# First-batch chunks, one early fold, a split load and an earlier order of steps at the head of a fused attention and feed-forward kernel

## The chip, the cores and the metric

One NeuronCore of a Trainium2 chip runs the whole program. The metric is device time in microseconds, the median of several executions. One of these executions is recorded by the hardware profiler; its trace and page are what is read here. PE is the matrix engine (PEld its weight loads), DVE the vector engine, ACT the scalar engine, POOL the GpSimd engine, which issues most of the loads here, and SP the queue that issues stores and transposes.

## The reference

Four batches of 6080 tokens with 256 channels go through a channel attention, then all 24320 tokens through a feed-forward layer of 2048 hidden units:

```
qn = q / (norm(q, axis=tokens) + 1e-6);  kn likewise
s  = kn.T @ qn / tau                      # 256 x 256 for each batch
a  = softmax(s)
x  = v @ a                                # (4*6080, 256)
h  = x @ w_in                             # 256 -> 2048
out = (s*relu(h)**2 + b) @ w_out          # 2048 -> 256
```

Inputs and outputs are float32, `tau` is 1.

## The kernel before

The attention matrix never meets v directly: it is folded into the weights, `wa = a @ w_in` (fp16, 256 x 2048, one for each batch), and then h = v @ wa. So the first batch's matrix must be ready before any feed-forward work can start, and the later batches' matrices are worked out beside the main loop.

**Head (first batch).** q and k are loaded in chunks, `chunks_first`: pairs (partitions, rows per partition). Before, these are eleven chunks of four rows, nine on 128 partitions and those at places 4 and 6 on 120, and two of two rows on 128. The first two come by SP and ACT in float32, the others by POOL, which casts to fp16 on the way. For each chunk PE adds to the Gram matrix `s_ps` (L152), DVE or ACT square q and k (L175 to L181), DVE folds the four squared rows to one (`fold`, L195) and adds them to the first chunk's (`into_first`, L209). The last three chunks (`NLATE`) are kept apart: for these all k loads come first, then all q loads, and their squares are not folded but summed by PE row for row (`unfolded`, `add_norms`, L242 for k, L246 for q). The sums become inverse norms by four ACT operations (L267), `scale` (L292) multiplies the Gram matrix with k's, and `exps` (L298) takes the exponentials. `first_block` works out the first 256 columns of `wa` (L341, L336), `folds` the rest (L325): blocks of 256 columns at 256, 512 and 768, and of 512 at 1024 and 1536, each in two halves m = 0 and 1. Each half is scaled out of PSUM by ACT (L318) or DVE (L320): m = 0 by ACT, but by DVE for the blocks at 512 and 768; m = 1 always by DVE.

POOL issues the loads in this order: k and q, the first group of v (`load_v(0)`), `w_in` in four loads (two halves of its first 512 columns, columns 512 to 1024, columns 1024 to 2048), the second group of v, the four pieces of `w_out`, the third group of v, the scalars. Eight of its loads can be in flight; each further one waits for the landing of the eighth before it.

**Main loop.** A group is 512 tokens; step s = 16 g + m works on hidden columns 128 m to 128 m + 127 of group g. `mm1` (L656) makes these hidden units, two matmuls of 512 columns for two halves of `wa`; two steps share one PSUM tile of `ps_h`, which has two buffers. After every odd step ACT takes the relu of both (`relu`, L666); then comes the square, g = r * r (L679 on DVE, L677 on ACT). Group 0 is `plain`: its output matmuls (L728) start at step 11. The other groups use a scheme with seven products (L824) that needs sums of squares (L751 to L757) on DVE.

The order of the work on each engine is the program's order, which `po` fixes. What stands where around the change:

- `FOLDS` gives the steps after which the eight halves from column 512 on are folded and scaled: 1, 1, 3, 3, 6, 6, 10, 10. Columns from 1024 are first used at step 8, from 1536 at step 12.
- Group 0's first four squares are put on DVE at steps 5, 6, 7 and 8, the others right behind their relu.
- At step 7 DVE casts the first piece of `w_out` (L553), at step 12 PE transposes the second group of v (L395) and DVE copies it (L397); from step 13 on DVE has the sums for the constant row and the combinations of `w_out`.
- `keep_busy` (L474) puts extra matmuls between the chunks of the head.

Of the kernel before, what the change touches and what calls it, by code (L numbers as in the profile page):

```python
# [9 lines left out]
FP16 = mybir.dt.float16  # L10
# [7 lines left out]
def kernel(  # L18
# [12 lines left out]
    nc = tc.nc  # L31
    P = 128

    B, N, C = q.shape
    Dff = moe_w_in.shape[1]
# [20 lines left out]
    def po(ins):  # L56

        tc.keep_in_program_order(ins)
        return ins

    def pool(name, bufs, **kw):
        return ctx.enter_context(tc.tile_pool(name=name, bufs=bufs, **kw))
# [6 lines left out]
    late_pool = pool("late_pool", NLATE)  # L69
# [25 lines left out]
    JC = 4  # L95
    NDIRECT = 2

    NSHORT = 120

    def make_chunks(shapes):  # L100
        chunks, at = [], 0
        for np_, j in shapes:
            chunks.append((at, np_, j))
            at += np_ * j
        assert at == N
        return chunks

    whole, rest = divmod(N, P * JC)
    chunks_later = make_chunks([(P, JC)] * whole + [(rest // JC, JC)])
    short = [(P, JC)] * (whole - 2) + [(P, 2)] * 2  # L110
    for at in (4, 6):
        short.insert(at, (NSHORT, JC))
    chunks_first = make_chunks(short)

    class Gram:

# [44 lines left out]
        def norm_ops(self, c):  # L161

            qc, kc = self.tiles[c]
            _, np_, jc = self.chunks[c]
            st = {}

            at_end = self.b == 0 and c >= len(self.chunks) - NLATE

            def squares(a, js):
                def f():  # L170
                    if "sq" not in st:
                        st["sq"] = (late_pool if at_end else sq_pool).tile(
                            [P, 2, JC, C], FP16, tag="sq", name="sq")
                    if a == 1 and at_end and c == len(self.chunks) - 1:
                        po(nc.vector.tensor_mul(  # L175
                            st["sq"][:np_, 1, js, :], kc[:np_, js, :], kc[:np_, js, :]))
                    elif a == 0 and (self.b > 0 or at_end or c % 2 == 0):
                        po(nc.vector.tensor_mul(  # L178
                            st["sq"][:np_, 0, js, :], qc[:np_, js, :], qc[:np_, js, :]))
                    else:  # L180
                        po(nc.scalar.activation(  # L181
                            out=st["sq"][:np_, a, js, :], in_=(qc, kc)[a][:np_, js, :],
                            func=AF.Square))
                return f

            def fold(half, arrays, last):
                def f():
                    src = st["f", 2 * half] if 2 * half < jc else st["sq"]
                    if ("f", half) not in st:
                        if last:  # L190
                            t = f3_pool.tile([P, 2, 1, C], FP16, tag="f3", name="f3")
                        else:
                            t = sq_pool.tile([P, 2, half, C], FP16, tag=f"f{half}", name="f")
                        st["f", half] = t
                    po(nc.vector.tensor_add(  # L195
                        st["f", half][:np_, arrays], src[:np_, arrays, :half, :],
                        src[:np_, arrays, half : 2 * half, :]))
                    if last and c == 0:
                        self.first = st["f", half]
                    if last and (c == 0 or self.b > 0 and c == len(self.chunks) - 1):  # L200
                        for rows in self.rows:
                            rows.append((st["f", half], np_, 1))
                return f

            def into_first():

                dst, src = self.first[:np_], st["f", 1][:np_]
                if self.b == 0:
                    po(nc.vector.tensor_add(dst, dst, src))  # L209
                else:  # L210
                    po(nc.gpsimd.dma_start(out=dst, in_=src, accum_op=ALU.add))  # L211

            def unfolded(a):
                self.rows[a].append((st["sq"], np_, jc))

            ops = []
            for h in range(0, jc, 4):
                js = slice(h, min(h + 4, jc))
                ops += [squares(1, js), squares(0, js)]
            if at_end:  # L220
                return ops + [unfolded]
            if jc == 8:
                ops += [fold(4, slice(0, 1), False), fold(4, slice(1, 2), False)]
            ops += [fold(2, slice(0, 2), False), fold(1, slice(0, 2), True)]
            return ops + [into_first] if 0 < c < len(self.chunks) - 1 else ops
# [149 lines left out]
    def group(g):  # L375
        t0 = g * TG
        return t0, min(TG, NT - t0) // P
# [60 lines left out]
    NW = 512  # L438
    w_in_rows = moe_w_in.rearrange("(co p) f -> p co f", p=P)

    def load_w_in(f0, f1, co=None):
        cs = slice(0, CH) if co is None else slice(co, co + 1)
        po(nc.gpsimd.dma_start(out=w_in16[:, cs, f0:f1], in_=w_in_rows[:, cs, f0:f1]))
# [2 lines left out]
    for co in range(CH):  # L446
        load_w_in(0, NW, co)
    load_w_in(NW, 2 * NW)
    load_w_in(2 * NW, Dff)
    w_out_rows = moe_w_out.rearrange("(fo p) d -> p fo d", p=P)  # L450
    load_v(1)

# [27 lines left out]
    late = range(NCH0 - NLATE, NCH0)  # L480
    for c in range(NCH0 - NLATE):
        ops = g0.norm_ops(c)
# [3 lines left out]
        if c == NCH0 - NLATE - 1:  # L486
            ops, last_sum = ops[:-1], ops[-1]
# [4 lines left out]
    ops = {c: g0.norm_ops(c) for c in late}  # L492
# [71 lines left out]
    def at_step(s, f):  # L564
        side.setdefault(int(s), []).append(f)
# [1 line left out]

    FIN = (0, 3, 5, 7, 9, 11, 13, 17, 19, 22)
    first_group = [b * N // TG for b in range(B)]
    FOLDS = (1, 1, 3, 3, 6, 6, 10, 10)  # L570
    for i, f in enumerate(folds[2:]):
        early.setdefault(FOLDS[i], []).append(f)
    at_step(14, lambda: po(nc.vector.tensor_scalar_mul(
# [87 lines left out]
    def relu(g, i):  # L661
        n = group(g)[1] * P
        if i % 2 == 0:
            r_tiles[g, i // 2] = rpool.tile([P, 2, 2, TG], FP16, tag="r16", name="r16")
        r16 = r_tiles[g, i // 2]
        po(nc.scalar.activation(out=r16[:, :, i % 2, :n], in_=h_tiles.pop((g, i))[:, :, :n],  # L666
                                func=AF.Relu))

    def square(g, i0, i1, engine):

        n = group(g)[1] * P
        if i0 == 0:
            g_tiles[g] = gpool.tile([P, 2, NP, TG], FP16, tag="g16", name="g16")
        src = r_tiles[g, i0 // 2][:, :, i0 % 2 : i0 % 2 + i1 - i0, :n]
        dst = g_tiles[g][:, :, i0:i1, :n]
        if engine is nc.scalar:
            po(nc.scalar.activation(out=dst, in_=src, func=AF.Square))  # L677
        else:
            po(nc.vector.tensor_mul(dst, src, src))  # L679
# [168 lines left out]
    for s in range(NS + FT):  # L848
        g, m = divmod(s, FT)
        if g < NG:  # L850
            mm1(g, m)
        for f in early.pop(s, []):
            f()

        if m == SHIFT and 0 < g and g - 1 not in plain:
            items = seven_items(g - 1)
            work.append((items, 8 if g == NG - 1 else 7))
        if work:
            items, n = work[0]
            for f in items[:n]:  # L860
                f()
            del items[:n]
            if not items:
                work.pop(0)
        for gp in plain:
            for mp in range(FT):
                if s == gp * FT + PLAG[gp] + (mp * 4 // 3 if gp == 0 else mp):
                    plain_mm2(gp, mp)
        if g < NG and m % 2 == 1:
            relu(g, m // 2)  # L870
            if g in plain:
                late = g > 0 and m // 2 % 2 == 0
                if g > 0 or m >= 9:
                    square(g, m // 2, m // 2 + 1, nc.scalar if late else nc.vector)
        if 5 <= s <= 8:
            square(0, s - 5, s - 4, nc.vector)
        if g < NG and g not in plain and m in SQUARES:
            square(g, *SQUARES[m])
        if g == NG - 1 and m in LAST:
            LAST[m]()  # L880
        elif m == 0 and 0 < g and g - 1 not in plain:
            square(g - 1, 6, 8, nc.vector)
        elif 0 < g and g - 1 not in plain and m in SUMS:
            sums_of(g - 1, SUMS[m])
        for f in side.pop(s, []):
            f()
# [34 lines left out]
```

## Time and profile before

| | |
|---|---|
| median of 4 executions | 719.4 us (719.37 to 719.85) |
| the profiled execution, time | 719.85 us |
| its span, first to last instruction | 718.1 us |
| busy, PE | 695.5 us (97%) |
| busy, DVE / ACT / POOL | 623.0 (87%) / 545.2 (76%) / 109.9 us (15%) |
| granted clock of PE | 1.00 |
| DMA, mean | 116 GB/s; busy share 90% or more in the first 7 of 40 slices |
| first matmul of the feed-forward part (L656) | 38.53 us |

The page divides the span in 40 slices of 18 us. Only the first two are not full for PE: the head is a wait for loads, and the rest is nearly all matmuls. A row of a chain gives a start, a length and what ran; a row of a group gives an engine, what it wrote from what, a count, the busy time and the mean of one.

### The profile page before, as it was taken

The numbers are of one execution on the slowest core, as the hardware profiler recorded it, in microseconds if no ns is written. First come the engines' busy times: TensorE is split into PE (matmuls) and PEld (weight loads), VectorE is DVE, ScalarE is ACT, GpSimd is POOL, SyncE is SP. The second block draws the span as 40 slices with busy tenths as digits, with TensorE's granted clock in tenths as the row PEclk, the third lists the DMA queues.
The fourth block names the chain that finished last, engine by engine and source line by source line (L and its number), as shares of the span: only waits on it lengthen the run. The fifth ranks groups of instructions, "written<-read, shape, count | busy, mean of one in ns | idle before, by whom it ended". The sixth has DMA issues, their size and how long they took to land.

```text
span 718.1 us, 17493 instructions
## 1 busy us (share of the span) xinstructions
PE 695.5 (97%) x7423; PEld 502.8 (70%) x7423; DVE 623.0 (87%) x875; ACT 545.2 (76%) x593; POOL 109.9 (15%) x188
## 2 busy tenths in 40 slices
PE   4599999999999999999999999999999999999998
PEld 2456777776677777777677777777668777777777
DVE  4879999988889999998888899998887888888886
ACT  5779877787777777778777778777877777777875
POOL 4532332201201222111010222110000000000000
PEclk9999999999999999999999999999999999999999
DMA  9999999636555878444773788843323333321201
GB/s 237 204 259 170 152 168 147 111 99 123 107 107 126 141 134 144 108 92 88 134 154 54 147 125 130 155 90 75 99 63 74 94 71 75 96 60 46 82 31 74
DMA packets 86990, 83.47 MB, mean 116 GB/s; under 512 B 56320, under 2 KB 61568, under 8 KB 86912
## 3 DMA queue, kind: packets, MB, share of 16 engines
q0 software_dynamic: 26144, 43.40, 37.5%
q1 hardware_dynamic: 60192, 37.64, 21.4%
q8 instruction: 58, 0.95, 0.6%
q10 hardware_dynamic: 576, 1.31, 0.5%
q14 instruction: 20, 0.16, 0.1%
HBM read 78.91 MB, written 24.90 MB: 145 GB/s over the span
## 4 chain that ended last, share of the span: by engine, by line
PE 92%; DMA 4%; DVE 2%; ACT 1%; POOL 1%; issue 0%; POOLq 0%; ACTq 0%
PE h_ps L656 45%; PE o_ps L824 40%; PE s_ps L152 4%; DMA qk<-in_k_dram 3%; PE wa_ps L325 2%; DMA v<-in_v_dram 1%; PE o_ps L728 1%; DVE g L679 0%; PE o_ps L702 0%; POOL qk L136 0%; ACT r L666 0%; DVE wa L320 0%; DVE o_sb L684 0%; DVE S L753 0%; DVE sq L178 0%
## 5 line engine op out<-in xcount | busy, mean ns | idle before, releaser
L666 ACT ACTIVATE r<-h_ps 128x1024 f16<-128x1024 f32 (+1 forms) x384 | 388.5, 1014 | 152.5 <-PE h_ps L656 148.6
L656 PE MATMUL h_ps<-vT,wa 128*128 128x512 f16 (+7 forms) x1632 | 452.4, 364 | 0.6 <-DVE wa L320 0.4
L824 PEld LDWEIGHTS <-S 128*128 128x128 f16 x2944 | 198.0, 98 | 84.8 <-issue 0.2
L824 PEld LDWEIGHTS <-g 128*128 128x128 f16 x2208 | 155.0, 98 | 74.1
L679 DVE TENSOR_TENSOR g<-r 128x2048 f16<-128x2048 f16 (+2 forms) x150 | 174.4, 1164 | 13.5 <-ACT r L666 12.9
L824 PE MATMUL o_ps<-T,S 128*128 128x128 f16 x2208 | 183.3, 219 | 0.1
L656 PEld LDWEIGHTS <-wa 128*128 128x128 f16 x1632 | 135.8, 98 | 21.2 <-DVE wa L320 1.3
L824 PE MATMUL o_ps<-w_out,g 128*128 128x128 f16 x1472 | 134.2, 219 | 0.2 <-DVE u L684 0.2
L684 DVE SCALAR_TENSOR_TENSOR o_sb<-o_ps,s_out,u 128x256 f32<-128x256 f32 x138 | 66.3, 481 | 50.9 <-PE o_ps L824 48.9
L677 ACT ACTIVATE g<-r 128x1024 f16<-128x1024 f16 (+1 forms) x97 | 100.4, 1035 | 0.2
L152 PE MATMUL s_ps<-qk 128*128 128x256 f16 (+2 forms) x384 | 70.0, 282 | 15.9 <-ACT qk L143 8.9
L384 POOL DMA_DIRECT2D v<-in_v_dram x48 | 31.5, 660 | 265.1 <-DMA vT<-v 214.2
L684 DVE SCALAR_TENSOR_TENSOR u<-o_ps,s_out,rowconst 128x256 f32<-128x256 f32 x138 | 65.8, 477 | 0.0
L824 PE MATMUL o_ps<-w_out,S 128*128 128x128 f16 x736 | 63.4, 219 | 0.0
L824 PE MATMUL o_ps<-N,g 128*128 128x128 f16 x736 | 63.4, 219 | 0.0
L211 POOL DMA_DIRECT2D f<-f x30 | 26.3, 876 | 225.4 <-DVE f L195 175.4
L753 DVE TENSOR_TENSOR S<-S,g 128x2048 f16<-128x2048 f16 (+1 forms) x47 | 56.4, 1201 | 1.3
L181 ACT ACTIVATE sq<-qk 128x1024 f16<-128x1024 f16 (+3 forms) x53 | 54.5, 1042 | 3.9 <-DMA qk<-in_k_dram 2.3
L751 DVE TENSOR_TENSOR S<-g 128x2048 f16<-128x2048 f16 (+1 forms) x47 | 56.0, 1192 | 0.0
L755 DVE TENSOR_TENSOR S<-g 128x2048 f16<-128x2048 f16 x46 | 55.9, 1214 | 0.0
L757 DVE TENSOR_TENSOR S<-g,S 128x2048 f16<-128x2048 f16 x46 | 55.9, 1214 | 0.0
L152 PEld LDWEIGHTS <-qk 128*128 128x128 f16 (+2 forms) x384 | 32.2, 101 | 21.9 <-ACT qk L143 9.4
(81 smaller groups left out, 312.6 us busy)
## 6 DMA issues: line engine op xcount, KB each, us to landing
out_dram<-o_sb SPq DMA_DIRECT2D x42, 512.0 KB, 2.9
v<-in_v_dram POOLq DMA_DIRECT2D x47, 256.0 KB, 4.7
qk<-in_k_dram POOLq DMA_DIRECT2D x40, 256.0 KB, 6.5
qk<-in_q_dram POOLq DMA_DIRECT2D x40, 256.0 KB, 7.5
f<-f POOLq DMA_DIRECT2D x30, 128.0 KB, 3.2
vT<-v SPq DMA_TRANSPOSE x182, 3.1
out_dram<-o_sb SPq DMA_DIRECT2D x10, 256.0 KB, 4.4
w<-in_moe_w_out_dram POOLq DMA_DIRECT2D x4, 512.0 KB, 10.2
```

Source lines behind the costliest of these rows:

```text
L152: po(nc.tensor.matmul(self.s_ps[:, ch, :], qc[:np_, j, ts(ch, P)], kc[:np_, j, :], start=(c == 0 and j == 0 and ch == 0), stop=(c == len(s ...
L181: po(nc.scalar.activation(out=st["sq"][:np_, a, js, :], in_=(qc, kc)[a][:np_, js, :], func=AF.Square))
L656: po(nc.tensor.matmul(dst, wa[:, ci, ts(m, P)], src, start=(ci == 0), stop=(ci == CH - 1), skip_group_check=True))
L666: po(nc.scalar.activation(out=r16[:, :, i % 2, :n], in_=h_tiles.pop((g, i))[:, :, :n], func=AF.Relu))
L677: po(nc.scalar.activation(out=dst, in_=src, func=AF.Square))
L679: po(nc.vector.tensor_mul(dst, src, src))
L684: po(nc.vector.scalar_tensor_tensor(out=dst, in0=src, scalar=s_out, op0=ALU.mult, in1=add, op1=ALU.add))
L751: po(nc.vector.tensor_add(T[1], A21, A22))
L753: po(nc.vector.tensor_sub(T[2], T[1], A11))
L755: po(nc.vector.tensor_sub(T[3], A11, A21))
L757: po(nc.vector.tensor_sub(T[4], A12, T[2]))
L824: po(nc.tensor.matmul(st[name][:, j, :], a()[:, i, ts(j, P)], w[:, i, :], start=first, stop=last, skip_group_check=True))
```

## The change

Four edits, all in the head and in the first ten steps of the main loop:

- `make_chunks` now takes the rows per partition alone and puts each chunk on 128 partitions while rows last. The first batch's chunks become eleven of four rows and one of two rows on 128 partitions, and a last one of two rows on 96. The later batches' chunks stay as they are.
- Of the three last chunks, the one with four rows gets a fold of its squares, once for k and once for q: DVE adds rows 0 and 1 to rows 2 and 3 in a new tile `h`, and PE sums two rows in place of four. In DVE's order k's add stands ahead of the last chunk's k square, q's add ahead of the two other q squares.
- `w_in`'s last 1024 columns come in two loads of 512.
- The blocks at 1024 and 1536 are folded at steps 5 and 8 instead of 6 and 10, and group 0's squares all stand right behind their relu, so the first four at steps 1, 3, 5 and 7. At step 5 the block's scaling thereby stands ahead of the step's relu on ACT.

PE's program has 12 instructions fewer (four ahead of the first late chunk's Gram matmuls, eight behind them), ACT's and DVE's work in the main loop is the same but in another order, POOL has one more load.

```diff
-    NSHORT = 120
-
-    def make_chunks(shapes):
+    def make_chunks(rows_of):
         chunks, at = [], 0
-        for np_, j in shapes:
+        for j in rows_of:
+            np_ = min(P, (N - at) // j)
             chunks.append((at, np_, j))
             at += np_ * j
...
-    whole, rest = divmod(N, P * JC)
-    chunks_later = make_chunks([(P, JC)] * whole + [(rest // JC, JC)])
-    short = [(P, JC)] * (whole - 2) + [(P, 2)] * 2
-    for at in (4, 6):
-        short.insert(at, (NSHORT, JC))
-    chunks_first = make_chunks(short)
+    whole = N // (P * JC)
+    chunks_first = make_chunks([JC] * whole + [2, 2])
+    chunks_later = make_chunks([JC] * (whole + 1))
...
+            if at_end and jc == 2:
+                return ops + [unfolded]
             if at_end:
-                return ops + [unfolded]
+                def half(a):
+                    if "h" not in st:
+                        st["h"] = late_pool.tile([P, 2, 2, C], FP16, tag="h", name="h")
+                    po(nc.vector.tensor_add(st["h"][:np_, a], st["sq"][:np_, a, :2],
+                                            st["sq"][:np_, a, 2:]))
+                    self.rows[a].append((st["h"], np_, 2))
+                return ops + [half]
...
-    load_w_in(2 * NW, Dff)
+    load_w_in(2 * NW, 3 * NW)
+    load_w_in(3 * NW, Dff)
...
-    FOLDS = (1, 1, 3, 3, 6, 6, 10, 10)
+    FOLDS = (1, 1, 3, 3, 5, 5, 8, 8)
...
                 late = g > 0 and m // 2 % 2 == 0
-                if g > 0 or m >= 9:
-                    square(g, m // 2, m // 2 + 1, nc.scalar if late else nc.vector)
-        if 5 <= s <= 8:
-            square(0, s - 5, s - 4, nc.vector)
+                square(g, m // 2, m // 2 + 1, nc.scalar if late else nc.vector)
```

## The prediction

> **What bounds the kernel now.** I read the busy shares by slice first, then the chain of waits with its pieces in order of time, then stretches cut at the chain's turning points, and last the timeline of DVE around steps 6 to 12.
>
> Stretches (PE, PEld, DVE, ACT, POOL busy us with counts, clock, DMA share, GB/s):
>
> ```profile
> 30.00:34.77 4.77, 3.71 (x44) 2.73 (x42) 2.99 (x7) 3.55 (x8) 3.74 (x6) 1.00 1.16 201
> 34.77:36.58 1.81, 0.00 (x0) 0.01 (x1) 0.75 (x2) 1.48 (x5) 0.27 (x1) 1.00 1.22 200
> 36.58:43.47 6.89, 6.89 (x48) 4.04 (x49) 4.13 (x10) 4.30 (x7) 3.66 (x6) 1.00 1.09 287
> 43.47:47.97 4.50, 4.01 (x19) 1.57 (x18) 4.42 (x7) 3.98 (x5) 1.59 (x3) 1.00 1.07 292
> 47.97:74.02 26.05, 25.70 (x196) 17.01 (x196) 24.31 (x41) 23.06 (x28) 5.95 (x12) 1.00 1.10 177
> 74.02:718.10 644.08, 640.84 (x7032) 467.71 (x7031) 567.61 (x769) 490.16 (x525) 81.06 (x132) 1.00 0.55 105
> ```
>
> From 74 us on PE has work for 640.84 of 644.08 us and the change touches nothing there, so all that can be won lies ahead of it: up to 36.58 PE waits for loads, then for 0.49 us between 43.47 and 47.97. From 47.97 to 74.02 PE, DVE and ACT are all nearly full; a start earlier by x passes through whole if all three start earlier by x.
>
> Pieces of the chain (start, us, what):
>
> ```profile
> 27.18 0.28 issue
> 27.47 9.06 DMA v<-in_v_dram
> 36.53 0.05 issue
> 36.58 0.62 PE vT_ps L395 x8
> ...
> 42.60 0.88 PE wa_ps L325 x4
> 43.47 0.02 issue
> 43.50 0.75 DVE wa L320
> 44.25 1.20 DVE g L679 x2
> 45.45 0.60 DVE w_out L553
> 46.05 1.20 DVE g L679 x2
> 47.25 0.67 DVE wa L320
> 47.92 0.05 issue
> 47.97 0.39 PE h_ps L656
> ```
>
> The head ends with the first v tile, landing at 36.53. The second bend is an order: at step 10 the scaling of the last `wa` block stands on DVE behind four squares and a cast, so PE gets it at 47.97.
>
> **The change part by part.** *Chunks.* In the trace's landing records a q or k load of 128 partitions follows the one before by 1.20 to 1.32 us, and one of 120 partitions by as much (1.22 to 1.28): of its sixteen landings fifteen come as always and one far ahead (13.74 against 15.14 and later). So 120 partitions cost what 128 cost. Before, k and q are 11 such units and two halves (0.61 to 0.65 us each); after, 11, one half and one of 96 partitions. No row has 96. If it goes in eights, as 120 did, it gains nothing; if evenly, a quarter of 0.62 us, 0.16 for k and 0.16 for q. The later batches' loads of 112 partitions have no landing ahead of the rest (279 us: 283.80 to 283.92 for fifteen), so they were split evenly; I take 0.31 us, with 0 as the other end. The Trainium skill (DMA: Bandwidth & Descriptors, the section on why a DMA increments its semaphore by 16) says that GpSimd's direct copies may put partitions/16, rounded up, on each engine: 120 leaves one engine out and 96 uses all; by it the gain would be the same 0.31. So the last q lands at 33.23 for 33.54, and all behind it earlier by as much.
>
> *One fold.* DVE gains two adds of 128x512 (425 ns each, L195's form), PE loses two matmuls of the k sums and four of the q sums (12 instructions with their weight loads). The k add lies in DVE's gap ahead of 32.33. The q add does not: from the landing of the first late q (32.14), 0.68 + 0.42 + 0.42 + 0.42 ends the squares at 34.1 for 33.99. It eats the earlier arrival: exps end at 36.41 for 36.35. Cost 0.06 us, and only where the exps end last.
>
> *What ends the head.* The v load was late by accident: fifteen landings came by 34.77, the sixteenth at 36.53. All its data packets had started by 34.4; between 34.5 and 35.5 stands one packet of another queue:
>
> ```profile
> q0 software_dynamic: 200, 0.18, 113.1%
> q8 instruction: 1, 0.02, 6.1%
> ```
>
> The page has 58 such loads for 7423 weight loads and 7423 matmuls, 256 instructions each: PE's program. It took 974 ns on one DMA engine and the landings behind it there are 1.1 to 1.8 us late: v 36.53, the two pieces of `w_in`'s first block 36.71 and 37.20 (others 35.47, 36.09). PE stood at its 256th instruction or so, just ahead of v's transposes. With 12 fewer it gets there after v's wait, so I expect the page to fall behind v, on `w_in`'s pieces: v at 34.5, second piece 37.20 - 0.31 = 36.9. Then `first_block`'s last two matmuls go at 36.95 for 37.66: gain 0.7. Bounds: 0.3 if the page hits v again (only the 0.31 arrives), 1.1 if it hits nothing that is waited for (exps at 36.41, matmuls at 36.5).
>
> *`w_in`'s end in two loads.* One issue more on POOL (L443's mean 0.63 us), a slot of eight in flight. Behind it wait v(1), the `w_out` pieces, v(2), the scalars. DMA has over 8 us queued, so nothing starves; nearest users: v(1) landed 42.28, used 48.63; v(2) at 49.18, its transposes land by 58.5 and are used at 65. Cost 0 to 0.1 on the path, I take 0. What it buys is cover: the third block is there by 39.5 for 41.0, and step 5 wants it at 42.0 less the gain above.
>
> *Order of steps.* In times of before: step 5 ends at 42.0, so the fold of block 1024 goes from 42.43 to 42.0. ACT's scaling began 0.69 after the fold, DVE's 1.07: 42.69 to 43.37 and 43.07 to 43.82. But the scaling is now ahead of step 5's relu on ACT, so that relu ends at 44.39 for 43.22, and step 8, which takes its PSUM buffer (`ps_h` has two), waits from 43.73 to 44.42: 0.69, against 0.4 to 0.5 that step 8 waited for DVE before. Step 8 then ends at 44.85 and fold 1536 follows at once, to 45.72. On DVE square 2, square 3 and the cast end by 46.7, the scaling by 47.45. PE does steps 9 to 11 and the first output matmuls (three times 0.43 and 0.44) by 47.46 and reaches the second half of step 12 at 47.6, with the block there. It was 47.97: gain 0.35; with ACT a little earlier (steps 1 and 3 start their relus at 39.60 and 40.90) up to 0.55. I take 0.4, low end 0.2. The four squares moved ahead of scalings wait for no late relu: square 0 has its relu at 40.62, the next scaling its matmuls at 41.1.
>
> **Sum.** The profiled execution took 719.85 (span 718.1 and 1.75 around it): 719.85 - 0.7 - 0.4 = 718.75. The three others took 719.37 to 719.42, and the median is 719.4. If their 0.45 is the page falling luckier on v, then 718.75 stands for all; if it is the profiling, 718.3. I take 718.5.
>
> **The rivals.** 0.2% is 1.44 us, about what a measurement can tell from no change; faster begins below 717.96.
>
> *1, forecast:* start 0.7, middle 0.4: 717.9 to 718.9. For it: the landings above. Chance 0.46 (0.06 faster, 0.40 same).
>
> *2, the page meets nothing:* start 1.1, middle 0.55, and of the 0.35 us that PE stands between 47.97 and 74.02 some goes too: 719.85 - 1.65 to 2.0, less 0 to 0.45: 717.4 to 718.2, with arrivals a little better 717.1. For it: 12 instructions fewer put the request behind v's wait. Against it: `w_in` is still queued when it comes. Chance 0.36 (0.34, 0.02).
>
> *3, slower: PE's clock.* The place is 30 to 37 us, where PE is busy 3.71 of 4.77 and 0 of 1.81 us; the change takes some 0.45 us of matmuls out and PE waits longer for the k add. The clock column reads 1.00 throughout, but the trace shows a slow PE: the first eight matmuls of 256 columns took 1.89 us at 7.03, the same eight 1.05 at 23.54. If PE runs `first_block` and the steps at that pace, 11 us of matmuls stretch by 0.8 per us for as long as it lasts: 3 us cost 2.4, the whole 11 us 8.8. From 2.6 us it outweighs the 1.1 gained by over 1.44: 720.9 and up. The Trainium skill (TensorE: Matmul & The Clock Gate, part 1) lets the clock fall after an idle window of about 3.4 us; by it this needs twice the gap seen, and the sum stays as it is. Against it: 1.81 us idle left the matmuls at 36.58 quick, and the gap gets shorter if v comes earlier. Chance 0.16 (0.15 slower, 0.01 same).
>
> *4, nothing:* v late as before, step 8's new wait takes the middle's gain: 719.0 to 719.6. Chance 0.02.
>
> Together: faster 0.40, same 0.45, slower 0.15. The range leaves out the end of case 2 below 717.1 and most of case 3: 717.1 to 720.9.
>
> **What would show it.** Right: v's transposes by 35.5, the `wa` matmuls of L325 begin at 37.0 to 37.3 for 37.98, PE's wait for DVE's `wa` at step 12 gone, a wait for ACT's relu at step 8 of 0.4 to 0.7, o_ps of L824 first at 72.9 for 74.02. Wrong: v or the last q landing over 1 us behind its fellows, or matmuls of 512 columns over 0.25 us apart after 37 us.

## The result, and the profile after

| | before | after |
|---|---|---|
| median | 719.99 us of 61 executions (719.36 to 721.72) | 718.95 us of 41 (718.75 to 719.22) |
| ratio of the means | | 0.9981, 95% interval 0.9977 to 0.9986 |
| the profiled execution, time and span | 719.85 and 718.1 us | 718.94 and 717.2 us |

The time fell by a fifth of a per cent, and the range, 717.1 to 720.9, held it. The executions of the kernel before lie in three groups: 21 of the 61 under 719.7, 16 from 719.7 to 720.1, 24 from 721.1 on. The four that the prediction knew were three of the first group and, profiled, one of the second. The changed kernel's lie in one group. So the change is worth 0.45 us against the lowest group of before, 0.91 between the two profiled ones, and 1.04 between the medians. Most of the experiments are about these differences.

Stretches of the changed kernel (columns as before: PE, PEld, DVE, ACT, POOL busy us with counts, clock, DMA share, GB/s), the last three cut 0.92 us earlier than those of before:

```profile
30.00:34.66 4.66, 3.29 (x38) 2.60 (x38) 3.72 (x9) 3.53 (x7) 3.94 (x6) 1.00 1.17 204
34.66:36.05 1.39, 0.91 (x11) 0.59 (x9) 1.13 (x3) 1.26 (x5) 0.80 (x2) 1.00 1.24 208
36.05:42.55 6.50, 5.82 (x37) 3.32 (x38) 4.31 (x11) 3.77 (x7) 3.26 (x6) 1.00 1.15 269
42.55:47.05 4.50, 4.11 (x22) 1.95 (x20) 3.65 (x6) 4.12 (x6) 1.58 (x4) 1.00 1.05 319
47.05:73.10 26.05, 25.71 (x197) 17.00 (x196) 24.70 (x42) 23.70 (x29) 6.38 (x13) 1.00 1.08 185
73.10:717.20 644.10, 640.84 (x7032) 467.70 (x7031) 567.60 (x769) 490.14 (x525) 81.04 (x132) 1.00 0.56 105
```

The last row has the same length and the same busy PE as before (644.10 for 644.08, 640.84 both times), and so has the one ahead of it, 26.05 us: what was won is won by 47 us and passes through whole. In the head PE is now at work on v's transposes between 34.66 and 36.05, where before it stood for 1.81 us with 0.00 busy.

Pieces of the chain (start, us, what):

```profile
29.85 0.28 issue
30.14 7.15 DMA w_in<-in_moe_w_in_dram
37.29 0.04 issue
37.33 0.38 PE wa_ps L345 x2
37.71 0.44 PE wa_ps L329 x4
...
41.70 0.45 PE wa_ps L329 x2
42.14 0.03 issue
42.17 0.69 ACT wa L322
42.86 0.92 ACT r L671
43.78 0.04 issue
43.82 0.59 PE h_ps L661 x2
```

The head no longer ends with v but with the second half of `w_in`'s first block, landing at 37.29. The order of steps no longer ends with DVE's scaling but with ACT's, and the relu queued behind it. The same two places in PE's timeline (start, us, engine, line, what; in brackets the idle time ahead and what ended it), and the first output matmul of the seven-product scheme with `w_out`:

```profile
37.33 0.38 PE L345 MATMUL wa_ps<-w_in,eT 128*128 128x256 f16 x2 [0.68 <-DMA w_in<-in_moe_w_in_dram]
43.82 0.59 PE L661 MATMUL h_ps<-vT,wa 128*128 128x512 f16 x2 [0.39 <-ACT r L671]
73.09 0.22 PE L829 MATMUL o_ps<-w_out,g 128*128 128x128 f16 x1 [0.21 <-DVE u L689]
```

73.09 stands for 74.02: 0.93 earlier. The blocks' folds (L329 here, L325 before) begin at 37.55 for 37.98, so 0.43 of it is the head and 0.50 the order of steps. The program page is in both traces; in 35.1 to 36.1 us of this one:

```profile
q0 software_dynamic: 195, 0.19, 115.0%
q8 instruction: 1, 0.02, 6.1%
```

It starts at 35.14 for 34.51, takes 975 ns, and delays the second `w_in` piece: fifteen of its landings come by 35.93, the sixteenth at 37.29. The trace does not name a landing's engine; that the late one is the page's is read from its lateness, here and in what follows.

### The profile page after: what moved, and what is told of

It is laid out like the page before. It is cut to its first block, busy times and chain, and to the rows that moved or that the text cites. A ratio compares the mean times of both kernels' runs of the same rounds, so it can differ in the third digit from the quotient of the medians.

```text
span 717.2 us, 17484 instructions
## 1 busy us (share of the span) xinstructions
PE 695.0 (97%) x7417; PEld 502.8 (70%) x7417; DVE 623.8 (87%) x877; ACT 545.1 (76%) x593; POOL 110.5 (15%) x189
## 4 chain that ended last, share of the span: by engine, by line
PE 92%; DMA 4%; DVE 2%; ACT 2%; issue 0%; DVEq 0%; ACTq 0%
PE h_ps L661 45%; PE o_ps L829 40%; PE s_ps L148 4%; PE wa_ps L329 2%; DMA qk<-in_k_dram 1%; DMA raw<-in_q_dram 1%; DMA w_in<-in_moe_w_in_dram 1%; PE o_ps L733 1%; ACT sq L177 1%; ACT r L671 1%; DVE f L191 1%; PE o_ps L707 0%; DVE sq L174 0%; DVE o_sb L689 0%; DVE S L758 0%
## 5 line engine op out<-in xcount | busy, mean ns | idle before, releaser
L148 PE MATMUL s_ps<-qk 128*128 128x256 f16 (+1 forms) x384 | 70.1, 283 | 15.7 <-ACT qk L139 9.1
L177 ACT ACTIVATE sq<-qk 128x1024 f16<-128x1024 f16 (+2 forms) x53 | 54.5, 1041 | 3.9 <-DMA qk<-in_k_dram 2.3
L148 PEld LDWEIGHTS <-qk 128*128 128x128 f16 (+1 forms) x384 | 32.2, 101 | 21.6 <-ACT qk L139 9.5
```

The source lines that it names most:

```text
L148: po(nc.tensor.matmul(self.s_ps[:, ch, :], qc[:np_, j, ts(ch, P)], kc[:np_, j, :], start=(c == 0 and j == 0 and ch == 0), stop=(c == len(s ...
L177: po(nc.scalar.activation(out=st["sq"][:np_, a, js, :], in_=(qc, kc)[a][:np_, js, :], func=AF.Square))
```

## The experiments

Theory A, the prediction's: head and order of steps are separate gains that add, and the head is set by which transfer PE's program page (the 16 KB of instructions, loaded each 256 PE instructions; "the page" below) stands in front of. The rivals B and C are named in each expectation, and a letter does not mean the same rival throughout. Each kernel ran 10 or 11 times beside its profile, and those sent together had the kernel before run beside them: 35 runs for the first four (median 719.56, 8 of them over 721), 35 for the next four (720.03, 11 over 721), 33 for the last four (719.57, 6 over 721).

**One part at a time.** *Order alone*: before, with

```diff
-    FOLDS = (1, 1, 3, 3, 6, 6, 10, 10)
+    FOLDS = (1, 1, 3, 3, 5, 5, 8, 8)
```

and the squares behind their relu.

> Only the order of steps is changed (folds of the last two wa blocks at steps 5 and 8, group 0's first four squares behind their relu). If the middle of the sum is right, PE's wait for DVE's wa at step 12 goes, one for ACT's relu at step 8 of 0.4 us comes, and each execution is 0.45 to 0.5 us faster than its like of the kernel before, whatever happened in its head; the spread of the kernel before (719.4 to 721.7 us) stays, since PE's program ahead of v's wait is the same: single times near 718.9, 719.4 and 720.8. If the order also decides where the spread comes from, the times lie together like those of the changed kernel.

Median 719.10 (718.85 to 721.0), ratio 0.9992, 0.9983 to 1.0002. The lowest group is at 718.85 to 719.1 for 719.3 to 719.7, 0.45 lower; two of 11 are at 720.8 and 721.0. So the order brings its 0.45 and does nothing for the spread. In its profiled run (719.26) the page starts at 35.16, 0.65 later than in the trace of before, although PE's program ahead of it is the same: the last q landing came 0.65 later too, at 34.20 for 33.54. So the page's start is to be read against the last q landing, 0.97 us behind it before and 0.96 here.

*One fold alone*: before, with `half` for the last four-row chunk.

> Only the late chunk's squares are folded once: 12 PE instructions fewer ahead of v's wait, two adds more on DVE. Theory A (PE's next program page is asked for ahead of v's wait before, behind it after): the page falls on w_in's first pieces, v lands with all its parts by 34.9 us, first_block's last matmuls wait for w_in at 37.2 to 37.6, and the times lie together within 0.4 us, at 719.2 to 719.5. Theory B (the 120-partition loads, which leave one DMA engine out, make the spread): the times spread over 2 us as before.

719.57 (719.49 to 719.83), ratio 0.9994, 0.9985 to 1.0002. The page comes at 35.48, 0.97 later than in the trace of before, v is whole by 35.27, and `w_in`'s second piece lands at 37.51. The last q landing came 0.44 later here (33.98), so of the 0.97 theory A's shift by 12 instructions is 0.53. No run is above 720, as theory A said; the median is 0.07 above its range, and 0.17 above that of the lowest group of before beside it (719.40).

*Chunks alone*: before, with the new `make_chunks`.

> Only the chunks are changed (all of 128 partitions, the last of 96). PE's program keeps its length, so by theory A the page still meets v: the times spread as before, 0.2 to 0.3 us lower each, since the last q lands 0.2 to 0.3 us earlier. By theory B the times lie together, near 719.1.

719.25 (719.16 to 719.53), ratio 0.9992, 0.9983 to 1.0001. It is 0.15 below the lowest group, and the spread is gone here too, although PE's program ahead of v keeps its length; theory A had said that it would stay, and theory B (the loads of 120 partitions make the spread) that it would go. But the fold alone keeps these loads and loses the spread as well, so they alone do not make it. The trace shows what changed: the data come earlier against the page. v is whole by 34.71, the page starts at 34.65 and falls on `w_in`'s first piece, 36.80 on its engine:

```profile
36.85 0.39 PE L337 MATMUL wa_ps<-w_in,eT 128*128 128x256 f16 x2 [0.68 <-DMA w_in<-in_moe_w_in_dram]
```

*Split alone*: before, with `w_in`'s end in two loads.

> Only w_in's last 1024 columns come in two loads. With the folds at steps 6 and 10 nothing waits for them, so all theories say no change, within 0.1 us, and the spread as before. If one more load in POOL's queue starves a later one, v(1)'s transposes at step 12 or the w_out cast at step 7 begin later and it is slower by that.

719.52 (719.25 to 721.5), ratio 1.0, 0.999 to 1.0011, four of 12 over 721.2: no change in either. Its profiled run, 719.25, shows what sets the lowest group apart from the profiled run of before (719.85): the page starts at 34.63, 0.12 later than there, and v is whole at 35.13 for 36.53. Against the lowest group the order (0.46), the chunks (0.15) and the fold (-0.17) add up to 0.44, near the 0.45 of the whole change.

**The page moved earlier.** Six matmuls of two columns, 12 PE instructions, behind the last but one of the early chunks, in the kernel before and in the changed one:

```diff
         keep_busy(FILL.get(c - NCH0, 0))
+        if c == NCH0 - NLATE - 2:
+            tiny_busy(6)
```

> The kernel before with six matmuls of two columns (12 PE instructions with their weight loads) ahead of the late chunks; nothing else changed and no work of its own worth 0.1 us. Theory A (PE's program page, the 256 instructions' boundary): the page is asked for some 0.5 us earlier against the loads, meets v on nearly every DMA engine, and the upper times become the rule: most executions at 719.8 to 721.5, the median over 720. Theory B (only the 120-partition loads matter): the same spread and shares as before, a third of the times near 721.3.

> The changed kernel with the same six small matmuls, so that its page boundary lies where the kernel before has it. Theory A: the page comes 0.5 to 0.7 us earlier, meets w_in's first piece or the end of v: like the kernel with the chunks alone plus the order's 0.45, 718.7 to 719.1, with single times up to 720.8 where it meets v. Theory B: no change, 718.8 to 719.2 with no outlier.

Before with them: 720.13 (719.88 to 720.6), ratio 0.9999, 0.9991 to 1.0008. The page comes at 32.72, 1.8 us earlier and not 0.5. PE had begun 207 matmuls and weight loads by then, where it had begun 260 in the trace of before, so the page does not follow their count alone; that PE waits for loads in between fits, but what asks for the page was not seen. It falls on the last q loads (33.23 and 33.82 on the other engines, 34.75 and 35.01 on its own), and PE waits for q:

```profile
34.80 0.61 PE L152 MATMUL s_ps<-qk 128*128 128x256 f16 x4 [0.87 <-DMA qk<-in_q_dram]
```

None of its runs is at 719.4 and none at 721.3: the two ends of before's spread are gone. The changed kernel with them: 719.68 (719.43 to 720.91), ratio 0.9996, 0.9987 to 1.0004, so 0.73 above the changed kernel and above theory A's range too: it had the page on `w_in` or the end of v, but it comes at 32.48 and PE waits for q here as well:

```profile
34.55 0.61 PE L148 MATMUL s_ps<-qk 128*128 128x256 f16 x4 [0.71 <-DMA qk<-in_q_dram]
```

v is whole at 35.91, the folds start at 37.97 for 37.55 and the first step at 38.62 for 38.06. So twelve instructions that compute nothing the kernel needs cost 0.7 us, and 0.56 of it stands in the trace at the first step, behind a page that comes at another time. Five of its 12 runs lie at 720.2 to 720.9, with granted clocks of 0.993 to 0.995; no profile caught one of these.

**PE kept busy while it waits for v**: before, with

```diff
+    keep_busy(4)
     transpose_v(0)
     keep_busy(1)
```

> The kernel before with four idle matmuls of 512 columns more in PE's wait for v. Theory C (the times near 721.3 are executions in which PE stood so long at v's wait that its clock fell to half for one window of 3.4 us): the times near 721.3 go, those near 719.4 and 719.9 stay; granted clocks of 0.995 and less get rarer. If instead 721.3 is v or the last q landing later still, a third of the times stays there.

719.56 (719.27 to 720.08), ratio 0.9991, 0.9982 to 0.9999: six runs at 719.3 to 719.6, five at 720.0 to 720.1, none at 721, where 11 of the 35 beside it were. PE's timeline:

```profile
34.73 1.26 PE L474 MATMUL idle_ps<-fill 128*128 128x512 f32 x4
35.84 0.62 PE L395 MATMUL vT_ps<-ident,v 128*128 128x128 f16 x8
```

If a third of the runs fell in that group by chance, 11 runs would miss it about once in 60. The page keeps its place, 1.1 us behind the last q landing, so it is not moved by these instructions. So before's group at 721.3 goes with the idle PE. In the 103 runs of before beside the experiments all 25 over 721 have a granted clock of 0.993 to 0.995; of the other 78, 66 have 0.997 to 1.000 and 12 have 0.994 or 0.995, so a low mean clock alone does not make the time. The reading that fits: at 719.4 the page misses v, at 720.0 it hits v, and at 721.3 it hits v and PE's clock falls after the gap. No profile caught a run of the last group, so the slow matmuls themselves were not seen there, and the cause of this group stays open.

**The head's last wait, by the loads**: the changed kernel, with `w_in`'s first block loaded as columns 0 to 255 and then 256 to 511, and the fold of the second half at step 0.

```diff
-    for co in range(CH):
-        load_w_in(0, NW, co)
+    load_w_in(0, 2 * P)
+    load_w_in(2 * P, NW)
...
-    for f in (first_block, *folds[:2]):
-        f()
+    first_block()
...
-    FOLDS = (1, 1, 3, 3, 5, 5, 8, 8)
+    FOLDS = (0, 0, 1, 1, 3, 3, 5, 5, 8, 8)
```

> The changed kernel with w_in's first block loaded in another cut: columns 0 to 255 of both halves first, then 256 to 511, and the block at 256 folded after step 0 instead of ahead of it. If what ends the head now is the DMA engine held up by the page on w_in's second piece (landing 37.29 for 35.93 elsewhere), then first_block needs only the first piece, lands by 35.3, its last matmuls go at 36.5 behind the exps, and mm1 starts at 37.2 for 38.06: 0.4 to 0.8 us faster than the changed kernel, 718.1 to 718.5. If the page meets the first piece instead, or step 2 waits for the block at 256, nothing is won: 718.9.

718.91 (718.70 to 719.12), ratio 0.9981, 0.9972 to 0.999: the changed kernel's time, and not the 718.1 to 718.5 expected. PE's timeline:

```profile
36.65 0.38 PE L345 MATMUL wa_ps<-w_in,eT 128*128 128x256 f16 x2
37.52 0.60 PE L660 MATMUL h_ps<-vT,wa 128*128 128x512 f16 x2 [0.49 <-ACT wa L322]
37.96 0.60 PE L329 MATMUL wa_ps<-w_in,eT 128*128 128x256 f16 x4
```

`first_block` no longer waits for a load and step 0 starts at 37.52 for 38.06. But now PE has nothing between `first_block` and ACT's scaling of it (0.49 us), where the changed kernel folds the next block; that fold is done later, and the block at 512 is folded at 38.83 for 38.94: 0.1 us is left of the 0.54.

**The page moved later.** The changed kernel with 8 and with 12 PE instructions fewer, taken from the extra matmuls between the chunks:

```diff
-    FILL = {-8: 1, -7: 1, -6: 1, -5: 2, -4: 2}
+    FILL = {-6: 1, -5: 1, -4: 1}
```

and `FILL = {-4: 1}`.

> The changed kernel with 4 of the 7 extra matmuls of the head left out (8 PE instructions fewer ahead of v's transposes; FILL one each behind the chunks at -6, -5 and -4). Theory A (PE's program page comes when PE's instruction count reaches a fixed point, 12 instructions ahead of where it now meets w_in's second piece): the page at 35.14 us moves past v's transposes to PE's wait for the exponentials, 35.9 us or later; w_in's second piece then lands at 36.0 on all engines, the second half of first_block starts at 36.5 for 37.33, and as ACT's scaling and the first step follow it, the first folds start at 36.8 to 37.0 for 37.55: 718.2 to 718.5. Theory B (the page comes at a time of its own, or w_in's piece is late for another reason): 718.95 as the changed kernel. Theory C (the extra matmuls carry PE's clock: without them it stands at half speed when the late chunks' sums and first_block come): each us at half speed in 31 to 38 us costs up to 0.8 us: 719.5 to 721.

> The changed kernel with 6 of the 7 extra matmuls of the head left out (12 PE instructions fewer; FILL one behind the chunk at -4). Theory A: the page comes behind PE's wait for the exponentials, at 36.1 us or later, and meets nothing that first_block waits for: 718.2 to 718.5, the same as with 8 fewer if 8 were enough, 0.4 better if they were not. Theory B: 718.95. Theory C: half speed for one or two more idle stretches of some 3.4 us than with 8 fewer: 720 to 722.

With 8 fewer: 719.11 (718.49 to 719.61), ratio 0.9986, 0.9977 to 0.9995. The page comes at 35.74, 0.6 later (0.3 of it because the last q landing came 0.3 later in this profile), and still hits the second piece (37.77 on its engine, 36.21 on the others); 8 were not enough, and theory A's 718.2 to 718.5 was missed. With 12 fewer: 718.71 (718.47 to 720.02), ratio 0.9988, 0.998 to 0.9997. The page comes at 36.28, while PE waits for the exponentials; the second piece has landed on all engines by 36.23, and PE's wait for it is gone:

```profile
36.96 0.38 PE L345 MATMUL wa_ps<-w_in,eT 128*128 128x256 f16 x2
37.17 0.60 PE L329 MATMUL wa_ps<-w_in,eT 128*128 128x256 f16 x4
```

In this profile (718.71) the first fold is 0.38 earlier than in the changed kernel's and the first step 0.24, though the exponentials end 0.44 later. Four of its 11 runs are at 718.47 to 718.53, 0.45 below the changed kernel's median, at the edge of theory A's range. But four others are at 719.48 to 720.02, with granted clocks of 0.990 to 0.993, the way of theory C, which had 720 to 722. The stretches of this kernel, with the clock in the third column from the right:

```profile
20.00:31.72 11.72, 6.30 (x34) 3.96 (x34) 10.44 (x22) 8.54 (x9) 5.41 (x10) 0.74 1.13 208
31.72:36.49 4.77, 4.20 (x46) 3.28 (x45) 3.66 (x9) 3.24 (x11) 3.75 (x7) 0.92 1.21 206
```

From 20 to 31.72 the changed kernel has 1.00; here it is 0.74, which costs little as long as PE waits for loads there: this execution is 0.23 shorter than the changed kernel's profiled one all the same. That in these four runs it lasted into the sums of the late chunks, and cost there what the page's move won, is read from their granted clocks; none was profiled. This is the lowest median of all kernels run, but not a version to keep.

Against the last q landing, the runs line up by PE's program. The page starts 0.8 to 1.1 us behind that landing with the program of before (before, order alone, split alone, PE kept busy), 1.2 with the chunks alone, 1.5 with the fold alone, 1.8 in the changed kernel and the three that keep its program up to v (the other cut of `w_in`, and the two halves of the order edit below), 2.1 with 8 fewer and 2.6 with 12 fewer; with 12 more it comes 1.0 to 1.1 us ahead of it (of the fifteen landings that it does not hold up).

**The two halves of the order edit.** The changed kernel with the old `FOLDS`, and the changed kernel with the old places of the squares:

> The changed kernel with the folds of columns 1024 and 1536 back at steps 6 and 10, the squares of group 0 still right behind their relu. Theory A (the wait at step 12 needs both: the late fold and the squares ahead of its scaling on DVE; either edit alone takes most of it away): 718.95 to 719.15, and no wait of PE for DVE's wa at step 12 of over 0.15 us. Theory B (only the fold's place counts): the wait of 0.4 to 0.5 us is back, 719.4 to 719.5.

> The changed kernel with group 0's first four squares back at steps 5 to 8, the folds still at steps 5 and 8. Theory A (either edit alone takes most of the wait away): 718.95 to 719.15. Theory B (only the fold's place counts): 718.95. Theory C (only the squares' place counts): PE waits 0.4 to 0.5 us for DVE's wa at step 12 or earlier, 719.4 to 719.5.

Old `FOLDS`: 719.51 (719.32 to 719.57), ratio 0.9997, 0.9988 to 1.0006. Old squares: 718.90 (718.80 to 719.10), ratio 0.9988, 0.9979 to 0.9996. PE's waits, the first two lines with the old `FOLDS`, the third with the old squares:

```profile
44.28 1.25 PE L661 MATMUL h_ps<-vT,wa 128*128 128x512 f16 x5 [0.42 <-DVE wa L324]
47.10 0.89 PE L661 MATMUL h_ps<-vT,wa 128*128 128x512 f16 x2
```

```profile
43.79 0.59 PE L661 MATMUL h_ps<-vT,wa 128*128 128x512 f16 x2 [0.40 <-ACT r L671]
```

Theory B: only the fold's place counts, the squares' edit is worth nothing. With the old `FOLDS` the wait for DVE at step 8 is back, and at 47.10 the two matmuls of step 12 take 0.89 us where other steps take 0.59, so PE loses 0.30 there too.

## Why the prediction was right or wrong

*What bounds the kernel* was right: the stretch from 73.10 on is unchanged to 0.02 us.

*Chunks.* The last q landed at 33.35 for 33.54 in the profiled runs, 0.19 and not 0.31, but its loads were also issued 0.12 later there, which makes 0.31: from its issue to its landing the last q takes 7.33 to 7.34 us in the five profiles with the old chunks and 7.02 to 7.03 in the seven with the new ones (the two in which the page held it up left out). So the last load, of 96 partitions, was a quarter shorter, as the prediction took it. Run alone, the chunks brought 0.15 us against the lowest group, and took v out of the page's way.

*One fold.* Right: the exponentials end at 36.40 for 36.35, although q came 0.19 earlier. Its other effect, 12 instructions, was foreseen as the thing that moves the page, and it did.

*What ends the head.* The mechanism was right, the term was mis-sized: 0.43 for 0.7. The prediction moved the second piece's landing, 37.20 with the page in front of it, earlier by the 0.31 of the chunks, to 36.9, as if the page kept its hour. But the page came 0.63 us later (35.14, and 0.8 later against the last q landing), still in front of that piece, which therefore landed at 37.29. So of its signs the start of the folds was missed, 37.55 for 37.0 to 37.3. Moving a packet that delays a queue moves the delay with it; the landing had to be worked out from the page's new start. The run with 12 instructions fewer shows the rest: 0.45 us more in its four best executions, with the page behind the piece.

*`w_in` in two loads.* Right: 719.52 for 719.56 when run alone.

*Order of steps.* Right in the size (0.50 in the profiles, 0.45 and 0.55 to 0.6 in the runs, for 0.4, bounds 0.2 to 0.55) and in the new wait: 0.39 us for ACT's relu at step 8, for 0.4 to 0.7. The prediction gave no share of it to the folds or the squares; the folds have all of it.

*The sum.* 719.85 less the 0.43 and 0.50 measured is 718.92, and the profiled execution took 718.94. The prediction then asked whether the 0.45 us between the profiled run of before and the three others was the page's luck on v or the profiling, and took a value between, 718.5. It was not the profiling: groups at 719.4 and 720.0 are there without a profile, so 718.75 was the value to take, and 718.95 is 0.2 above it. That the medians differ by 1.04 where 719.4 to 718.5 made 0.9 is luck: the median of before moved up by 0.6 with the group at 721.3, which no term of the sum held, and against the lowest group the gain is 0.45, half of what was forecast.

*The rivals.* "The page meets nothing" is what the run with 12 instructions fewer comes to in its best executions, 718.47. The 717.4 to 718.2 given for it, and the end of 717.1, were too low: in that profile PE then waits 0.58 us for the exponentials and 0.40 for ACT's relu at step 8. "Slower: PE's clock" did not come to pass. By the granted clocks and the run with PE kept busy it may be at work in the kernel before, as the 1.3 us of 24 of the 61 executions; the four times that the prediction had held none of these.

The Trainium skill (TensorE: Matmul & The Clock Gate, part 1) has the clock fall after an idle window of about 3.4 us that runs on its own, so that its phase against the kernel varies from run to run. Ten of the fourteen profiles show such a stretch in the head: a half clock for 3.41 or 6.83 us, somewhere between 20.8 and 32.5 us, where PE also waits for loads. The length and the varying place agree with the page. That the window ahead must be idle does not, as the kernel with the old `FOLDS` shows:

```profile
17.59:21.00 3.41, 1.28 (x9) 0.89 (x9) 3.20 (x7) 2.64 (x4) 1.48 (x3) 1.00 1.12 210
21.00:24.41 3.41, 2.89 (x12) 1.80 (x13) 3.20 (x7) 2.54 (x3) 1.48 (x4) 0.50 1.11 208
```

PE is busy for 1.28 us of the 3.41 ahead of it, and the changed kernel, with the same 1.28 us there, keeps 1.00; the measurement decides. So the prediction's sentence from this page, that the loss needs twice the gap of 1.81 us, is thus no bound: PE need not stand all that time. No profile shows the stretches of the executions over 721. The same skill (Runtime: NRT & Kernel Launch, instruction fetch mechanics) calls the crossing of a 16 KiB block mostly hidden. For PE's supply of instructions nothing here speaks against that, but the data queued behind the block were 1.4 us late, and the measurement decides.

## What to carry to other kernels

When one of a load's sixteen landings alone is late, look for a page of instructions in front of it, and cost an edit also by the instructions that it adds or takes ahead of that point, computing or not. Work out the new place of such a page first, and the landings from it after. Where a few executions lie far apart, the median of four says little: ask what each group is before choosing the base of the sum.

## What the runs showed of the hardware that was not expected

- Twelve PE instructions that do no useful work cost the changed kernel 0.73 us, and moved the page by 2.7 us (35.14 to 32.48); 12 fewer moved it by 1.1 us (to 36.28), 0.3 of it with the loads. It starts when PE has begun 254 to 266 matmuls and weight loads in twelve profiles, but 207 and 203 in the two with 12 more.
- A transfer whose fifteen other landings are in can be held for 1.4 us by one page packet of 975 ns (35.93 and 37.29).
- The kernel before, whose profile has a gap of 1.8 us in PE, loses some 1.3 us in a third of its executions (49 of 164 in all comparisons lie over 721), and four matmuls in the gap took these away in 11 runs.
- PE's clock can fall to half for 3.41 us though PE was busy for 1.28 of the 3.41 us before. Where PE waits for loads, 3.41 us of it cost nothing that shows: with the old squares the profiled execution has them at 21 to 25 us and took 718.90, and the executions with a granted clock of 1.000 took 718.80 to 719.10.
